# Two steps near the end of a fused attention and expert kernel change places, and the preparation of its leftover pair is reordered

## The chip, the cores and the metric

The kernel runs on one core of a Trainium2 chip. The metric is device time in microseconds (us), the median over runs. Engines are named as in the profile: PE (TensorE matmul, PEld its weight loads), DVE (VectorE), ACT (ScalarE), POOL (GpSimd), SP (SyncE, which here only issues transfers). A "q" behind an engine's name is its sequencer.

## What is computed

Eight batches of 384 tokens go through attention with 16 heads that share one set of keys and values. The result, as 3072 rows of 1024 numbers, goes through a two-stage gate: each row picks one of 4 groups, and in it one of 4 experts. Each row is then multiplied through its expert's two weight matrices.

```python
scores = scale * np.matmul(q, k.transpose(0, 1, 3, 2))      # q: 8 x 16 x 384 x 64, k: 8 x 1 x 384 x 64
attn = softmax(scores)
x = np.matmul(attn, v)                                       # reshaped to 3072 x 1024
g_idx = argmax(x @ w_group); e_idx = argmax(xg @ w_expert[g])
h = np.maximum(xg[mask_e] @ w1[g, e], 0.0)
out[tok_idx] = combined[:, None] * (h @ w2[g, e])            # combined: the product of both gate weights
```

With these inputs nearly all tokens of a batch choose the same expert. The kernel relies on that, and has a path for what is left over.

## The kernel before, in words

**Pairs.** The attention is cut into 24 steps that the code numbers `p`; p = 3b + st is third `st` (128 tokens) of batch `b`. Two consecutive steps are interleaved: the loop body of line 576 computes the scores of step p (`scores`, PE, then an exponential on ACT) while it multiplies the weights of the step before it with the values (`values`, PE). Scores and values alternate in six blocks j = 0 to 5. DVE adds up the exponentials (`pre_add`, five additions of 128x1024), inverts the sums (`invert`), and at the end of the body `weigh` scales the finished attention output of the step before: DVE writes it in fp32 to the tile `xT` (line 300), POOL casts it to bf16 in the tile `xbf` (line 301). After the last third of a batch, SP stores `xbf` to the DRAM buffer `x_bf`.

**Tiles that matter.** `xT` is one tile for all batches, overwritten third by third. `xbf` has two buffers, one per batch in turn. The PSUM tiles of scores, gates, counts and expert products all rotate through three buffers (`side`).

**Expert units.** For each batch the expert that the first 128 tokens choose most often is applied to all 384 tokens. That is 14 units of PE work (`moe_units`, line 398): 8 `h_unit`s (first matrix, 8 matmuls of 128x384 each, whose moving operand is the whole `xbf` of the batch) and 6 `y_unit`s (second matrix). `fill(n)` runs the next n units. They are run in phases behind every third step (`PHASES`, line 523): behind step 3b + 1 the 14 units of batch b - 1. Behind step 22, the last phase, only the 8 h units of batch 6 are run (line 525). Its 6 y units and all 14 units of batch 7 follow behind the loop, around the values of the last step and the leftover pair.

**Gate.** `gate_a(b, lo, hi)` is 64 small matmuls over thirds lo to hi of `xT`. `choose_a` and `counts(b, None)` find the expert of batch b from its first third (DVE, PE, ACT, DVE), and `choose_b` (line 349) has POOL read the index and issue the loads of both weight matrices (four pieces of `w1`, one `w2`). `gate_math` computes the gate of all three thirds and `gate_c`, called by `counts(None, b)`, what goes with the chosen expert. In a phase, one `gates(b)` serves both: `xT` then holds the first third of batch b and the other two of batch b - 1.

**Leftover pair.** `early_pair` (line 536) picks one pair of batch and expert that has tokens left over. Its weights are loaded by `leftover_w1` and `leftover_w2`. Behind the loop the tokens of that batch are read back from `x_bf` into the tile `xe` (line 656); the up to 32 tokens concerned are ranked (`pr`, `rk`, `pick`, `pg`), gathered (`pb` transposes, `px`), sent through both matrices (`ph`, `py`) and scattered to their rows. All this is written out by hand between `fill` calls, so that an engine's queue holds exactly the order of the code. Two computations that belong to a safety check, `bound_a` and `bound_b` (two transposes `pq` on PE), stand among it.

The program ends with three more units, an indirect store of the leftover rows (line 755), and a branch that is not taken here.

## Time and profile before

| | |
|---|---|
| median of 3 runs | 463.39 us (463.28 to 463.78) |
| span of the profiled execution | 462.4 us |
| PE busy | 449.4 us (97%) |
| DVE busy | 308.8 us (67%) |
| ACT busy | 241.6 us (52%) |
| POOL busy | 60.4 us (13%) |
| last matmul ends | 454.59 us |

The profile page gives busy times by engine and the costliest groups of instructions. In a timeline, each line has the start of a run of like instructions, its length, the engine, the line of the code, the tile written and those read, the count, and in brackets how long the engine stood idle before and for what. A line of the list of waits gives the total, the number and the longest. PE's busy time is modelled and pipelined matmuls overlap, so a group's cost is best read as the distance from its start to the start of the next group.

### The profile page before, as it was taken

The numbers are of one execution on the slowest core, as the hardware profiler recorded it, in microseconds if no ns is written. First come the engines' busy times: TensorE is split into PE (matmuls) and PEld (weight loads), VectorE is DVE, ScalarE is ACT, GpSimd is POOL, SyncE is SP. The second block draws the span as 40 slices with busy tenths as digits, with TensorE's granted clock in tenths as the row PEclk, the third lists the DMA queues.
The fourth block names the chain that finished last, engine by engine and source line by source line (L and its number), as shares of the span: only waits on it lengthen the run. The fifth ranks groups of instructions, "written<-read, shape, count | busy, mean of one in ns | idle before, by whom it ended". The sixth has DMA issues, their size and how long they took to land. (4 is left out here: it accounts for less than half of the span.)

```text
span 462.4 us, 10190 instructions
## 1 busy us (share of the span) xinstructions
PE 449.4 (97%) x4196; PEld 200.4 (43%) x4208; DVE 308.8 (67%) x489; ACT 241.6 (52%) x345; POOL 60.4 (13%) x83
## 2 busy tenths in 40 slices
PE   8999999999999999999999999999999999999893
PEld 6334445333643345433543336433453335434551
DVE  4899965499708985199834997089852999554511
ACT  2966643676347743566436763477435664532231
POOL 1004003000210103000030002101030001501000
PEclk9999999999999999999999999999999999999998
DMA  8688997997599296993979566992969910999952
GB/s 164 92 141 116 217 215 106 262 191 150 95 197 251 53 205 93 246 197 89 152 121 272 109 139 106 216 243 44 199 100 252 188 69 2 162 217 268 270 134 104
DMA packets 152454, 74.55 MB, mean 161 GB/s; under 512 B 120256, under 2 KB 138944, under 8 KB 152400
## 3 DMA queue, kind: packets, MB, share of 16 engines
q0 software_dynamic: 28416, 37.81, 48.0%
q1 hardware_dynamic: 122656, 35.68, 33.0%
q8 instruction: 35, 0.57, 0.5%
q10 hardware_dynamic: 1328, 0.33, 0.4%
q14 instruction: 19, 0.16, 0.1%
HBM read 92.62 MB, written 19.01 MB: 241 GB/s over the span
## 5 line engine op out<-in xcount | busy, mean ns | idle before, releaser
L253 ACT ACTIVATE pt<-s 128x1024 f32<-128x1024 f32 x144 | 142.1, 1026 | 71.9 <-PE s L251 71.2
L251 PE MATMUL s<-qT,kT 64*64 64x512 f32 x1152 | 142.4, 594 | 0.3 <-ACT qT L229 0.2
L290 PE MATMUL o<-pt,v 64*64 64x512 f32 x1152 | 141.1, 590 | 0.0
L261 DVE TENSOR_TENSOR presum<-presum,pt 128x1024 f32<-128x1024 f32 x96 | 116.6, 1215 | 15.2 <-ACT pt L253 9.8
L407 PE MATMUL hps<-xbf,w 128*128 128x384 bf16 x512 | 87.3, 326 | 0.4 <-ACT hT L408 0.4
L417 PE MATMUL yps<-w,hT 128*128 128x512 bf16 (+1 forms) x380 | 84.6, 375 | 0.6
L259 DVE TENSOR_TENSOR presum<-pt 128x1024 f32<-128x1024 f32 x24 | 29.4, 1223 | 76.8 <-ACT pt L253 75.4
L290 PEld LDWEIGHTS o<-pt,v 64*64 64x64 f32 x1152 | 43.4, 133 | 76.8 <-issue 73.0
L251 PEld LDWEIGHTS s<-qT,kT 64*64 64x64 f32 x1152 | 40.8, 133 | 66.8 <-issue 60.0
L407 PEld LDWEIGHTS <-w 128*128 128x128 bf16 x512 | 48.1, 98 | 38.1 <-issue 7.3
L301 POOL CAST xbf<-xT 128x1024 bf16<-128x1024 f32 x24 | 25.0, 1041 | 302.7 <-DVE xT L300 302.7
L419 ACT ACTIVATE y<-yps,gsel 128x512 f32<-128x512 f32 x46 | 31.6, 687 | 56.9 <-PE yps L417 55.3
L408 ACT ACTIVATE hT<-hps 128x384 bf16<-128x384 f32 x64 | 31.2, 488 | 55.6 <-PE hps L407 52.4
L417 PEld LDWEIGHTS <-hT 128*128 128x128 bf16 x392 | 37.7, 98 | 44.6 <-issue 2.4
L145 POOL DMA_DIRECT2D w<-in_moe_w_dram x36 | 24.8, 707 | 58.1 <-DVE gsel L395 37.7
L300 DVE TENSOR_TENSOR xT<-o,rinv 128x1024 f32<-128x1024 f32 x24 | 29.2, 1215 | 2.5 <-PE o L290 2.5
L280 DVE STREAM_TRANSPOSE rinv<-rc 128x1024 f32<-128x1024 f32 x24 | 29.9, 1245 | 0.8
L265 DVE TRANSPOSE_TENSOR_REDUCE fold<-presum 128x32 f32<-128x1024 f32 x24 | 29.6, 1232 | 0.0
L243 DVE STREAM_TRANSPOSE qT<-qraw 128x1024 f32<-128x1024 f32 x20 | 23.6, 1202 | 0.0
L209 ACT ACTIVATE qraw<-qraw 128x1024 f32<-128x1024 f32 x21 | 22.0, 1049 | 0.0
L273 PEld LDWEIGHTS sm<-fold,sel 64*64 64x64 f32 x192 | 7.3, 133 | 13.3 <-issue 13.3
L312 PE MATMUL gps<-xT,gw 128*32 128x96 f32 (+2 forms) x576 | 12.6, 239 | 0.0
(152 smaller groups left out, 152.9 us busy)
## 6 DMA issues: line engine op xcount, KB each, us to landing
w<-in_moe_w_dram POOLq DMA_DIRECT2D x36, 512.0 KB, 11.3
w<-in_moe_w_dram POOLq DMA_DIRECT2D x9, 2048.0 KB, 25.9
out_dram<-y SPq DMA_DIRECT2D x23, 512.0 KB, 6.9
qraw<-in_q_dram SPq DMA_DIRECT2D x56, 192.0 KB, 3.6
x_bf<-xbf SPq DMA_DIRECT2D x8, 768.0 KB, 4.0
v<-in_v_dram SPq DMA_DIRECT2D x16, 96.0 KB, 3.1
k<-in_k_dram SPq DMA_DIRECT2D x28, 48.0 KB, 2.7
qn<-in_q_dram SPq DMA_DIRECT2D x4, 256.0 KB, 5.2
```

Of the source, the lines that this page charges most:

```text
L251: nc.tensor.matmul(out=ps[64 * c:64 * c + 64, a, :], lhsT=kT[b][r, j * D:(j + 1) * D], rhs=qT[p][r, c * CW:(c + 1) * CW], start=True, stop ...
L253: nc.scalar.activation(out=t[:], in_=ps[:], func=ACTF.Exp, scale=scale)
L259: nc.vector.tensor_add(out=presum[p][:], in0=pt[p, 0][:], in1=pt[p, 1][:])
L261: nc.vector.tensor_add(out=presum[p][:], in0=presum[p][:], in1=pt[p, j][:])
L265: nc.vector.tensor_reduce(out=fold[p][:], in_=presum[p][:].rearrange("p a (n i) -> p (a n) i", i=32), axis=AX, op=OP.add, apply_transpose= ...
L280: nc.vector.transpose(out=t[:].rearrange("p (b i) -> p b i", i=32), in_=rc[:].rearrange("p c b -> p (c b)").unsqueeze(2).to_broadcast([P, ...
L290: nc.tensor.matmul(out=o_ps[p][64 * a:64 * a + 64, c, :], lhsT=v_sb[b][r, j, :], rhs=pt[p, j][r, a, :], start=(j == 0), stop=(j == KB - 1))
L300: nc.vector.tensor_mul(out=xT[b][:, :, ts], in0=o_ps[p][:].rearrange("p c (h n) -> p (c h) n", n=P), in1=rinv[p][:].rearrange("p (h n) -> ...
L407: nc.tensor.matmul(out=ps[:, 0:S], lhsT=w1[:, ko, fc * P:(fc + 1) * P], rhs=xb[:, ko, :], start=(ko == 0), stop=(ko == KO - 1))
L408: nc.scalar.activation(out=state["h"][:, fc, :], in_=ps[:, 0:S], func=ACTF.Relu)
L417: nc.tensor.matmul(out=ps[:], lhsT=state["h"][:, fo, st * P:(st + 1) * P], rhs=w2[:, fo, cs], start=(fo == 0), stop=(fo == FO - 1))
L419: nc.scalar.activation(out=y, in_=ps[:], func=ACTF.Copy, scale=gs_of()[:, st:st + 1])
```

## The change

Steps 20 and 21 change places: the first third of batch 7 now runs before the last third of batch 6. The choice of batch 7's expert moves from the last phase into the body of step 22, in the form that step 2 already has for batch 0. With this the loads of its weights can be issued earlier, and only the rest of batch 6's gate stays in the phase.

```diff
+    def rest_of_gates(b):
+        gate_logits(b, gate_a(b, 1, ST), 1, ST)
+        gate_math(b)
...
-    for p in range(NP):
+    order = list(range(NP - 4)) + [NP - 3, NP - 4, NP - 2, NP - 1]
+    for prev, p in zip([None] + order, order):
         b, st = divmod(p, ST)
-        jobs = [lambda: gates(0), lambda: None, lambda: counts(0, None)] if p == 2 else []
+        jobs = []
+        if p == 2 or p == NP - 2:
+            jobs = [lambda: choose_a(b, gate_a(b, 0, 1)), lambda: None, lambda: counts(b, None)]
...
             if b == B - 1:
-                steps = {1: lambda: gates(b), 2: lambda: counts(b, None), 3: lambda: (counts(None, b - 1), early_pair())}
+                steps = {2: lambda: rest_of_gates(b - 1), 4: lambda: (counts(None, b - 1), early_pair())}
```

Everywhere else in the loop `p - 1` becomes `prev`. Behind the loop the preparation of the leftover pair is put in another order, so that each step on PE has at least one unit of other work between it and the step that makes its input:

```diff
-    fill(3)
+    bound_a()
+    fill(2)
+    bound_b()
+    fill(1)
     for j in range(KB):
...
     weigh(NP - 1)
     last = B - 1
-    fill(2)
-    gate_logits(last, gate_a(last, 1, ST), 1, ST)
-    gate_math(last)
-    bound_a()
-    fill(2)
-    counts(None, last)
-    bound_b()
-
     xe = pool.tile([P, KO, S], BF16, tag="qraw", bufs=2, name="xe")
     nc.sync.dma_start(out=xe[:].rearrange("p k s -> p (k s)"), in_=xb_dram[bass.ds(leftover["b"], 1)].rearrange("a p k -> (a p) k"))
+    fill(2)
+    rest_of_gates(last)
...
-    nfl = pool.tile([P, 1], FP32, tag="nfl", bufs=1, name="nfl")
-    nc.vector.reduce_sum(out=nfl[:], in_=extra[:], axis=AX)
-    fill(1)
+    fill(2)
     pr = side([P, CW], FP32, "pr")
...
+    of_last = pool.tile([P, 2, P], FP32, tag="presum", bufs=1, name="of_last")
+    nc.vector.tensor_scalar(out=of_last[:, 0, :], in0=pick[:, ST - 1, :], scalar1=leftover["final"][:, 0:1], scalar2=None, op0=OP.mult)
     pick_bf = pool.tile([P, ST, CAP], BF16, tag="kT", name="pick_bf")
     nc.vector.tensor_copy(out=pick_bf[:], in_=pick[:, :, 0:CAP])
...
-    fill(2)
+    fill(1)
+    counts(None, last)
+    nfl = pool.tile([P, 1], FP32, tag="nfl", bufs=1, name="nfl")
+    nc.vector.reduce_sum(out=nfl[:], in_=extra[:], axis=AX)
+    fill(1)
     pg = side([P, CW], FP32, "pg")
     for st in range(ST):
         nc.tensor.matmul(out=pg[:, 0:2], lhsT=pick[:, st, :], rhs=gi[:, st, :], start=(st == 0), stop=(st == ST - 1))
+    nc.tensor.transpose(out=pg[:, P:2 * P], in_=of_last[:, 0, :], identity=ident[:])
...
-    nc.tensor.transpose(out=pg[:, P:2 * P], in_=of_last[:, 0, :], identity=ident[:])
...
-    fill(1)
     xtok = []
     for st in range(ST):
+        fill(1)
         pb = side([P, Dm], BF16, "pb")
...
-        fill(1)
-    assert len(units) == 2 * ST
+    fill(1)
     px = side([P, KO, CAP], FP32, "px")
...
     leftover["yc"] = yc
-    fill(1)
+    fill(2)
     spread()
```

## The prediction

> **What bounds the kernel now.** I read the page's busy times first, then PE's list of waits, then the timeline around the two places the diff touches.

> ```profile
> PE 449.4 (97%) x4196; PEld 200.4 (43%) x4208; DVE 308.8 (67%) x489; ACT 241.6 (52%) x345; POOL 60.4 (13%) x83
> ```
> ```profile
> PE pr L672 <- DVE mb L664: 1.2, 1, 1.2
> PE pb L717 <- DMA xe<-x_bf: 0.8, 1, 0.8
> PE hps L407 <- ACT hT L408: 0.4, 1, 0.4
> PE pg L698 <- DVE gc L694: 0.4, 1, 0.4
> ```

> PE is the bound: past the first 8 us it waits four times, 2.8 us in all, and all four lie in the leftover preparation. So time changes only by PE work added, by these waits closed, or by a new wait on PE. The tail behind the loop on PE:

> ```profile
> 421.12 1.10 PE L312 MATMUL gps<-xT,gw 128*32 128x64 f32 x64
> 422.15 1.90 PE L417 MATMUL yps<-w,hT 128*128 128x512 bf16 x7
> ...
> 425.21 0.38 PE L512 MATMUL pq<-ident,sq 128*1 128x128 f32 x2
> 425.99 1.46 PE L407 MATMUL hps<-xbf,w 128*128 128x384 bf16 x8 [0.39 <-ACT hT L408]
> 428.65 0.18 PE L672 MATMUL pr<-mb,prefix 128*128 128x4 bf16 x1 [1.20 <-DVE mb L664]
> ...
> 432.69 0.33 PE L698 MATMUL pg<-ident,of_last 128*128 128x128 f32 x1 [0.37 <-DVE gc L694]
> ...
> 435.15 0.62 PE L717 MATMUL pb<-ident_bf,xe 128*128 128x128 bf16 x8 [0.83 <-DMA xe<-x_bf]
> ```

> The body of step 22 and the phase behind it, where PE never stops:

> ```profile
> 373.62 2.75 PE L251 MATMUL s<-qT,kT 64*64 64x512 f32 x24
> ...
> 384.15 2.77 PE L407 MATMUL hps<-xbf,w 128*128 128x384 bf16 x16
> 386.85 1.53 PE L312 MATMUL gps<-xT,gw 128*32 128x96 f32 x64
> 388.31 1.47 PE L407 MATMUL hps<-xbf,w 128*128 128x384 bf16 x8
> ```

> The body takes 384.15 - 373.62 = 10.53 us. The first h unit of batch 6 starts at once, because that batch's last third was weighed a whole body earlier. At the end of this body DVE and POOL weigh step 21:

> ```profile
> 384.79 1.22 DVE L300 TENSOR_TENSOR xT<-o,rinv 128x1024 f32<-128x1024 f32 x1
> ```
> ```profile
> 386.07 1.04 POOL L301 CAST xbf<-xT 128x1024 bf16<-128x1024 f32 x1 [9.38 <-DVE xT L300]
> ```

> The cast ends at 387.11, 2.96 us after PE has left the body. Nobody needs it there now.

> [...] So a waiting first h unit holds everything behind it; the trace agrees, PE's groups follow the code's order. [...] Here the last matmul ends at 454.59 and the granted clock still is 1.00 up to 459, then 0.62 in the next microsecond, so it fell about 4.6 us later; a gap of 3 us should not trip it. [...] All 24 casts took 1.04 us[...].

> **Part 1, the swap: a new wait.** Now step 20 precedes step 22, so the body of step 22 ends with the weighing of step 20, the last third of batch 6. The h units of batch 6 follow directly and read all of `xbf`. PE must stand until values -> xT -> cast is done. Nothing else is queued ahead of that unit on PE; all 8 h units, the gate and the next step's scores stand behind it.

> **Part 2, the choice moved into step 22.** Step 2 has the same body with the same jobs, so I read its price there:

> ```profile
> 26.67 2.75 PE L251 MATMUL s<-qT,kT 64*64 64x512 f32 x24
> 29.36 0.76 PE L312 MATMUL gps<-xT,gw 128*32 128x32 f32 x64
> ...
> 33.65 0.18 PE L338 MATMUL cps<-ohe,ones_bf 128*128 128x16 bf16 x1
> ```
> ```profile
> 38.02 1.18 DVE L261 TENSOR_TENSOR presum<-presum,pt 128x1024 f32<-128x1024 f32 x1
> ```

> Step 2's body runs from 26.67 to 39.59, 12.92 us. From it I take the transposes `qps` that step 22 lacks (36.80 to 37.82, and 0.11 for the switch): 11.8 us. Against 10.53 that is +1.27: 0.69 for the gate's matmuls, 0.11 for the count, 0.17 where the last scores wait for a PSUM buffer, the rest in changes of shape.

> On DVE, step 2's last addition starts 11.35 us into the body and ends at 12.5. In step 22 the chain is the same (choice 0.75, index 0.46, five additions, inversion), so xT runs from 12.5 to 13.7 and the cast from 13.75 to 14.8. POOL must first issue batch 7's five loads: in step 2 the index was ready 8.75 into the body and POOL finished issuing at 13.96; in six of the other seven batches it finished 4.7 after the index, here 13.45. So POOL is free between 13.45 and 13.96, and the cast ends between 14.8 and 15.05. I take 14.8, and 0.1 for the hand-over: the first h unit starts 14.9 into the body instead of 10.53, **+4.35 us**, of which 1.27 is Part 2 and 3.1 idle PE (bounds 2.7, if DVE gains 0.4 on step 2, and 3.4).

> **Part 3, the phase.** The gate of 96 columns (386.85 to 388.31, 1.46) becomes one of 64 (421.12 to 422.15, 1.03): **-0.43**. Its input, xT of step 20, is there three h units earlier. `early_pair` moves back one unit; its DVE work ends about where the phase ends, and step 23's first addition comes 3 us later, so nothing waits.

> **Part 4, the earlier loads.** Today batch 7's loads are issued from 392.78 and the leftover weights queue behind them. No weight tile is in PE's list of waits, so arriving 9 us sooner is worth nothing by itself. It empties the DMA engines before the tail, which is where `x_bf` (7.8 us to land there, 3.4 at best) and `xe` (7.0) were slow.

> **Part 5, the tail.** Start to start: `pq` 425.21 to 425.99 is 0.78, alone some 0.35, so -0.4. h at 425.99 plus 1.30 is 427.29, `pr` at 428.65: -1.35. `pg` to its transpose 431.59 to 432.69 is 1.10, in one go some 0.65: -0.45. h at 432.85 plus 1.30, `pb` at 435.15: -1.0. Sum 3.2. Does each close? `pr` now comes one y and one h unit (1.74 + 1.30) behind the gate. DVE's chain from gate to `mb` is 2.2 us (422.28 to 424.51) and another 0.65 (428.01 to 428.59, with the hand-over), 2.9 after 422.28, so `mb` is there at the moment PE arrives: closed, with 0.1 to spare at most. `xe` is issued when `x_bf` has landed: 3.5 + 4 us behind the store, about 428 in the old tail's time against a `pb` at 430.5: closed if the transfers run as on an empty bus. I take **-3.1**, with bounds -2.3 (xe late by 0.8) and -3.4. What follows `y` unit 3 (spread, two units, the indirect store) keeps its order and its 12 us.

> **Sum:** +4.35 - 0.43 - 3.1 = +0.82, so 463.39 + 0.8 = **464.2 us**, 0.17% more.

> **Rivals.** *Slower:* the cast has to wait for POOL's loads (+0.25), and the tail closes only 2.3, for `xe` or `mb` (+0.8): +1.9, 465.3 us. For it: step 2's slow issue, and `mb` without slack. Against it: six of the eight issues are quicker and the DMA engines are less loaded. *Faster:* PE does not wait for the cast, because something I overlook fills the gap, and only +1.27 - 0.43 - 3.1 = -2.3 remains, 461.1 us. For it: PE has not one such idle stretch now. Against it: the h unit's operand is the whole `xbf`, and no unit of batch 5 is left at that point (its 14 are used up behind step 19). *Loads decide:* if batch 7's weights had been the limit, the swap would pay; the list of waits has no such line, so I give it nothing apart from `xe`.

> **How the numbers follow.** The balanced case has 70% and spreads over 463.5 to 464.9 with the bounds of Parts 2 and 5. The bound of 0.2% is 0.93 us, that is 464.32, just above its middle: 0.46 of it count as no change and 0.24 as slower. The slower rival has 20%, the faster one 8%, and 2% are left for what I don't see (no change). Chances: faster 0.08, no change 0.48, slower 0.44. The range goes from 463.0 to 465.4; the faster rival and half of the outer slower cases lie outside.

> **What would show it.** Right: PE's list of waits has a new line of about 3 us, h unit on POOL's cast, right behind step 22; the phase behind is 0.4 shorter; the four waits of the tail are gone, or under 0.3 in sum; the loads start near 383.5. Wrong: no such wait, or a wait over 3.6 with a fallen clock; `pb` still on `xe`; a new wait of `py` on the second leftover weights, which are now needed some 5 us sooner after their issue.

## The result, and the profile after

The changed kernel takes 466.26 us (median of 6 runs, 465.43 to 466.8) against 463.58 us before (463.08 to 463.78): ratio 1.0058, 95% interval 1.0046 to 1.0071. It is slower by 2.7 us, outside the range of 463.0 to 465.4 that was forecast. The profiled execution is the quickest of the six, with a span of 463.9 us (465.43 us of device time) against 462.4 (463.94) before.

First the busy times of the profile after, then PE's list of waits behind the first 8 us (total, times, longest):

```profile
PE 450.4 (97%) x4272; PEld 200.4 (43%) x4272; DVE 308.3 (66%) x489; ACT 241.9 (52%) x345; POOL 60.5 (13%) x83
```
```profile
PE hps L407 <- POOL xbf L301: 2.9, 1, 2.9
PE py L749 <- DMA w<-in_moe_w_dram: 1.5, 1, 1.5
```

The four waits of the tail are gone. Two others stand in their place: the first h unit of batch 6 on POOL's cast, and `py`, the leftover pair's second product, on its weights.

PE's timeline in the body of step 22 and the phase behind it:

```profile
373.69 2.75 PE L251 MATMUL s<-qT,kT 64*64 64x512 f32 x24
376.38 0.76 PE L312 MATMUL gps<-xT,gw 128*32 128x32 f32 x64
...
380.67 0.18 PE L338 MATMUL cps<-ohe,ones_bf 128*128 128x16 bf16 x1
...
388.51 4.06 PE L407 MATMUL hps<-xbf,w 128*128 128x384 bf16 x24 [2.91 <-POOL xbf L301]
392.50 1.10 PE L312 MATMUL gps<-xT,gw 128*32 128x64 f32 x64
...
400.16 2.81 PE L251 MATMUL s<-qT,kT 64*64 64x512 f32 x24
```

What it waits for, in DVE's and then in POOL's timeline:

```profile
386.14 1.21 DVE L300 TENSOR_TENSOR xT<-o,rinv 128x1024 f32<-128x1024 f32 x1
```
```profile
383.49 2.73 POOL L145 DMA_DIRECT2D w<-in_moe_w_dram  x4 [6.72 <-issue]
386.18 0.93 POOL L357 DMA_DIRECT2D w<-in_moe_w_dram  x1
387.41 1.04 POOL L301 CAST xbf<-xT 128x1024 bf16<-128x1024 f32 x1 [0.31 <-DVE xT L300]
```

The first h unit starts 388.51 - 373.69 = 14.82 us into the body; before it was 10.53. The next step's scores begin at 400.16, which is 3.90 us later than in the kernel before:

```profile
396.26 2.81 PE L251 MATMUL s<-qT,kT 64*64 64x512 f32 x24
```

POOL was done with its five loads at 387.11, and xT was ready at 387.35, so the loads did not hold the cast.

The tail on PE's timeline:

```profile
425.23 1.10 PE L312 MATMUL gps<-xT,gw 128*32 128x64 f32 x64
...
429.31 0.18 PE L671 MATMUL pr<-mb,prefix 128*128 128x4 bf16 x1
...
434.30 0.61 PE L718 MATMUL pb<-ident_bf,xe 128*128 128x128 bf16 x8
...
444.38 1.89 PE L417 MATMUL yps<-w,hT 128*128 128x512 bf16 x8
447.79 1.06 PE L749 MATMUL py<-w,hc 128*32 128x256 bf16 x32 [1.53 <-DMA w<-in_moe_w_dram]
...
452.99 3.65 PE L417 MATMUL yps<-w,hT 128*128 128x512 bf16 x24
```

The load that `py` waits for, on POOL's timeline, and the time from its issue to its landing, after and before:

```profile
428.99 0.89 POOL L575 DMA_DIRECT2D w<-in_moe_w_dram  x1 [4.79 <-PE yps L417]
```
```profile
DMA to landing us min/median/max: 18.7/18.7/18.7
```
```profile
DMA to landing us min/median/max: 20.8/20.8/20.8
```

`pr` and `pb` no longer wait. A y unit takes 1.74 us, so PE was ready for `py` at 446.12 and lost 1.67. From the scores of step 23 to the end of the last matmul it is 400.16 to 456.64, 56.48 us; before it was 396.26 to 454.59, 58.33. The tail thus gained 1.85: 3.5 from the closed waits, less 1.67. With the loop's 3.90 the last matmul comes 2.05 later. What follows it took 7.3 us instead of 7.8, which leaves the span's +1.5.

That is not the 2.7 us of the medians. Of the 1.2 us between them, 0.4 is that the profiled execution of the kernel before was itself slower than its median (463.94 against 463.58). The other 0.8 is in the list of the six executions. Each has a mean granted clock, the share of TensorE's full speed that the profile records, averaged over the execution. The profiled one, at 465.43, has 0.998; the others take 465.91 to 466.80 at 0.991 to 0.994. The experiments had to say what costs that clock.

### The profile page after: what moved, and what is told of

Read it like the earlier page. It is cut to its first block, busy times and chain, and to the rows that moved or that the text cites. A ratio compares the mean times of both kernels' runs of the same rounds, so it can differ in the third digit from the quotient of the medians.

```text
span 463.9 us, 10326 instructions
## 1 busy us (share of the span) xinstructions
PE 450.4 (97%) x4272; PEld 200.4 (43%) x4272; DVE 308.3 (66%) x489; ACT 241.9 (52%) x345; POOL 60.5 (13%) x83
## 5 line engine op out<-in xcount | busy, mean ns | idle before, releaser
L251 PE MATMUL s<-qT,kT 64*64 64x512 f32 x1152 | 142.7, 594 | 0.0
L261 DVE TENSOR_TENSOR presum<-presum,pt 128x1024 f32<-128x1024 f32 x96 | 116.6, 1215 | 14.9 <-ACT pt L253 9.5
L407 PE MATMUL hps<-xbf,w 128*128 128x384 bf16 x512 | 87.2, 326 | 2.9 <-POOL xbf L301 2.9
L417 PE MATMUL yps<-w,hT 128*128 128x512 bf16 (+1 forms) x392 | 85.2, 375 | 0.0
L251 PEld LDWEIGHTS s<-qT,kT 64*64 64x64 f32 x1152 | 40.8, 133 | 66.9 <-issue 60.2
L407 PEld LDWEIGHTS <-w 128*128 128x128 bf16 x512 | 48.1, 98 | 40.3 <-issue 9.6
L301 POOL CAST xbf<-xT 128x1024 bf16<-128x1024 f32 x24 | 25.0, 1043 | 293.7 <-DVE xT L300 293.7
L408 ACT ACTIVATE hT<-hps 128x384 bf16<-128x384 f32 x64 | 31.3, 489 | 56.1 <-PE hps L407 51.4
L417 PEld LDWEIGHTS <-hT 128*128 128x128 bf16 x392 | 37.8, 98 | 44.6 <-issue 2.4
L300 DVE TENSOR_TENSOR xT<-o,rinv 128x1024 f32<-128x1024 f32 x24 | 29.2, 1215 | 2.5 <-PE o L290 2.5
L318 DVE STREAM_TRANSPOSE L<-gps 128x32 f32<-128x32 f32 (+1 forms) x16 | 3.7, 228 | 16.5 <-PE gps L312 16.5
```

Source lines behind the costliest of these rows:

```text
L251: nc.tensor.matmul(out=ps[64 * c:64 * c + 64, a, :], lhsT=kT[b][r, j * D:(j + 1) * D], rhs=qT[p][r, c * CW:(c + 1) * CW], start=True, stop ...
L261: nc.vector.tensor_add(out=presum[p][:], in0=presum[p][:], in1=pt[p, j][:])
L300: nc.vector.tensor_mul(out=xT[b][:, :, ts], in0=o_ps[p][:].rearrange("p c (h n) -> p (c h) n", n=P), in1=rinv[p][:].rearrange("p (h n) -> ...
L407: nc.tensor.matmul(out=ps[:, 0:S], lhsT=w1[:, ko, fc * P:(fc + 1) * P], rhs=xb[:, ko, :], start=(ko == 0), stop=(ko == KO - 1))
L408: nc.scalar.activation(out=state["h"][:, fc, :], in_=ps[:, 0:S], func=ACTF.Relu)
L417: nc.tensor.matmul(out=ps[:], lhsT=state["h"][:, fo, st * P:(st + 1) * P], rhs=w2[:, fo, cs], start=(fo == 0), stop=(fo == FO - 1))
```

## The experiments

The theory after the result: PE's pieces are +3.90 in the loop, -3.5 in the tail and +1.7 for the new wait of `py`; on top of it, the idle stretch of 2.9 us at the cast makes the granted clock fall in many executions, against what the prediction had said. The rival: the additional time and the lower clock come from elsewhere. "Before" is each time the kernel before, run beside the experiments on the same chip.

**The changed kernel once more,** without an edit.

> The changed kernel once more, unaltered. In its first trace PE's pieces sum to +2.05 us at the last matmul (loop and phase +3.90, new wait of py on the second leftover weights +1.6, tail gaps -3.45) and the span grows by 1.5 us, but the median over six runs grew by 2.7 us, and the runs with more time show a lower mean clock (0.991 to 0.994 against 0.998). Theory: PE's new idle stretches let the granted clock fall for a few us in most executions; then the median is again 466 to 466.6, and a run with a clock near 0.992 shows matmuls at half speed right behind one of the two waits. Rival: the extra 0.8 us has nothing to do with these waits (the end of the program, other work on the chip); then the clock falls elsewhere or not at all while the time stays near 466.3.

Measured: 466.39 us (463.65 to 467.81, 8 runs) against 463.79, ratio 1.0048 (1.0027 to 1.0069). This time the profiled execution is one with a low clock, 0.991. PE's timeline and wait, and busy times by stretches of 2 us (PE, PEld, DVE, ACT, POOL, granted clock, DMA share, GB/s):

```profile
388.87 5.47 PE L407 MATMUL hps<-xbf,w 128*128 128x384 bf16 x24 [2.90 <-POOL xbf L301]
394.27 1.10 PE L312 MATMUL gps<-xT,gw 128*32 128x64 f32 x64
```
```profile
388.00:390.00 2.00, 1.13 (x4) 0.55 (x4) 1.99 (x2) 0.00 (x0) 0.82 (x1) 0.59 1.14 179
390.00:392.00 2.00, 2.00 (x8) 0.96 (x7) 0.00 (x0) 0.38 (x1) 0.00 (x0) 0.56 1.10 158
```
```profile
PE py L749 <- DMA w<-in_moe_w_dram: 0.2, 1, 0.2
```

The three h units behind the wait take 394.27 - 388.87 = 5.40 us instead of 3.99: the clock is at about half between 388 and 392, and nowhere else before the end of the program. That is the theory's picture. Not all eight executions fit it: the slowest, 467.81 us, has a clock of 0.995, and its excess is not explained. Two with a clock of 0.996 take 463.65 and 464.18, about as long as the kernel before.

The `py` wait is 0.2 here instead of 1.5. `pr` comes 1.76 us later than in the first trace (431.07 against 429.31), `py` only 0.48 (448.27 against 447.79). If the issue of its weights moved with `pr`, they landed some 17.4 us behind it instead of 18.7, an estimate from these starts (18.7 - 1.76 + 0.48); why is not shown.

**Only the loop's part.** The tail is that of the kernel before; the edit is shown against that kernel.

```diff
-    for p in range(NP):
+    order = list(range(NP - 4)) + [NP - 3, NP - 4, NP - 2, NP - 1]
+    for prev, p in zip([None] + order, order):
...
-                steps = {1: lambda: gates(b), 2: lambda: counts(b, None), 3: lambda: (counts(None, b - 1), early_pair())}
+                steps = {2: lambda: rest_of_gates(b - 1), 4: lambda: (counts(None, b - 1), early_pair())}
```

> Only the loop's part of the change: steps 20 and 21 swapped, the choice moved into step 22, the tail as before. Theory: loop and phase +3.9 us, of it 2.9 idle on the cast; the earlier loads free the DMA engines, so the wait of pb on xe (1.0 with its start) goes, and py has its old 22 us behind the issue of its weights, so it does not wait: 463.6 + 2.9 = 466.5 us by the pieces, and 467.3 if the idle stretch at the cast is what costs clock. Rival (the clock is lost at the py wait): 466.5 with a clock as in the kernel before.

Measured: 467.22 us (465.78 to 470.15, 6 runs), ratio 1.0087 (1.0065 to 1.0109). Three executions have a clock of 0.997 or more and take 465.8 to 466.7, three have 0.992 or 0.993 and take 467.7 to 470.2. From the profiled execution (clock 0.998), PE's timeline:

```profile
388.58 4.06 PE L407 MATMUL hps<-xbf,w 128*128 128x384 bf16 x24 [2.91 <-POOL xbf L301]
...
438.12 0.61 PE L721 MATMUL pb<-ident_bf,xe 128*128 128x128 bf16 x8
...
450.44 1.06 PE L753 MATMUL py<-w,hc 128*32 128x256 bf16 x32
```

`pb` and `py` do not wait, and still the clock falls in half of the executions. So the wait of `py` is not needed for the fall. By itself the loop's part loses 3.4 us, as the theory had it with the clock.

**Only the tail's part.** The loop is that of the kernel before; the edit is shown against the changed kernel.

```diff
-    order = list(range(NP - 4)) + [NP - 3, NP - 4, NP - 2, NP - 1]
-    for prev, p in zip([None] + order, order):
+    for p in range(NP):
...
```

> Only the tail's reordering, the loop as before, so no swap, no early choice. Theory: the tail's waits on hT, mb and gc close (-2.4 us), pb on xe perhaps not, as the leftover weights still queue behind batch 7's, and py arrives some 3 us before its weights, which landed at 445.7 before: net between -0.3 and +0.7, 463.3 to 464.3 us, with a wait of py of 2 to 3 us. Rival (the earlier loads buy nothing in the tail): all four waits close and py does not wait, 460.2 us.

Measured: 466.98 us (466.39 to 468.2, 6 runs), ratio 1.0075 (1.0061 to 1.0089). The theory missed by about 3 us and the rival by almost 7. PE's timeline, SP's timeline, and the stretches of 2 us:

```profile
435.95 0.62 PE L718 MATMUL pb<-ident_bf,xe 128*128 128x128 bf16 x8 [4.79 <-DMA xe<-x_bf]
436.40 2.66 PE L407 MATMUL hps<-xbf,w 128*128 128x384 bf16 x8
438.86 1.06 PE L718 MATMUL pb<-ident_bf,xe 128*128 128x128 bf16 x8
```
```profile
420.92 0.33 SPq L303 DMA_DIRECT2D x_bf<-xbf  x1
428.59 0.36 SPq L655 DMA_DIRECT2D xe<-x_bf  x1
```
```profile
436.00:438.00 2.00, 2.00 (x14) 1.19 (x15) 0.69 (x1) 0.00 (x0) 0.00 (x0) 0.63 1.07 305
```

`x_bf` lands 7.5 us behind its issue and `xe` 7.3 behind its own, much as before (7.8 and 7.0): the DMA share is 1.06 to 1.25 in every stretch of 2 us from 410 to 436, where in the changed kernel it is 0.00 to 0.52 from 422 to 428. In the trace before, the last piece of the leftover `w1`, issued at 398.97, took 36.7 us to land. But the new order asks for `xe` at 431.0. So PE waits 4.8 us where it waited 0.8, and behind that the clock is at half again: an h unit takes 2.46 instead of 1.30. I had taken the old wait of 0.8 as what was at stake; the tail's other gains only bring PE to the same transfer earlier. The two halves of the change need each other: in the changed kernel `x_bf` lands in 3.4 us, `xe` in 5.2, and `pb` finds it.

**One y unit ahead of `py`.** The changed kernel, with the unit that it had moved behind `py` put back in front.

```diff
     nc.vector.tensor_copy(out=hc[:], in_=phT[:])
-    fill(1)
+    fill(2)
...
     leftover["yc"] = yc
-    fill(2)
+    fill(1)
```

> The changed kernel with one y unit (1.74 us) moved from behind py to ahead of it, where it stood before. Theory: py comes 1.74 us later than today and its weights have landed, so the wait of 1.5 is gone and nothing is added: 466.3 - 1.6 = 464.7 us. If the py wait is also what costs clock, 463.9. Rival (the weights are later when other work precedes them, or the store of the middle third, now issued at the same place, sets the end): no more than 0.5 us gained, 465.8.

Measured: 465.83 us (463.68 to 466.43, 6 runs), ratio 1.0047 (1.0034 to 1.0060). The profiled execution has a clock of 0.997 and is the one at 463.68; the five others have 0.991 to 0.993. On PE's timeline the wait is gone:

```profile
444.38 3.62 PE L417 MATMUL yps<-w,hT 128*128 128x512 bf16 x16
447.93 1.06 PE L749 MATMUL py<-w,hc 128*32 128x256 bf16 x32
```

The median is that of the rival (465.8), though not for its reason: the wait did go, but the clock still falls. The edit is worth hardly 0.6 us on the median, measured beside the changed kernel's 466.39. In the three traces with both halves of the change and no y unit put back (the changed kernel's two, and the one below with PE kept busy) the wait of `py` is 1.5, 0.2 and 0.3 us; the 1.5 of the first trace, which the theory counted on, is the upper end. To see executions with and without a fallen clock side by side the kernel was run again.

> The kernel with the y unit ahead of py once more, for a trace of an execution in which the clock fell: five of its six executions took 465.6 to 466.4 us at a clock of 0.991 to 0.993, the sixth 463.7 at 0.997. Theory: all of the 2.2 us between them is h units at half clock behind the wait for the cast; three h units then take some 6 us instead of 4.0 and nothing later differs. Rival: the half clock costs only the 1.4 us seen in the changed kernel's second trace, and the other 0.8 lies elsewhere, in a second fall or in transfers that land later.

Measured: 464.67 us (463.36 to 466.62, 20 runs), ratio 1.0024 (1.0009 to 1.0038). Ten executions have a clock of 0.996 or more and take 463.36 to 464.38, ten have 0.990 to 0.994 and take 464.95 to 466.62. Their medians are 463.57 and 466.07: executions with a fallen clock take 2.5 us longer here. The profiled one had a full clock, so the question of this run, where the part beyond the 1.4 us seen in the h units lies, stays open.

**PE kept busy in the wait.** The changed kernel with matmuls that nobody reads, placed into PE's wait for the cast.

```diff
             if b == B - 1:
+                busy = side([P, CW], FP32, "busy")
+                for _ in range(44):
+                    nc.tensor.matmul(out=busy[:, 0:P], lhsT=ones_bf[:], rhs=ones_bf[:], start=True, stop=True)
                 steps = {2: lambda: rest_of_gates(b - 1), 4: lambda: (counts(None, b - 1), early_pair())}
```

> The changed kernel with 44 extra matmuls of 128x128 ones into a PSUM tile that nobody reads, ahead of the first h unit of batch 6, some 2.5 us that fit into PE's 2.9 us of waiting for the cast. No useful work is moved. Theory (the idle PE lets the granted clock fall to half, for some 3.4 us, in most executions): the clock is 0.997 or more in all executions and the time that of the changed kernel's best traces, 465.0 to 465.6 us. Rival (the clock falls for another reason, or the spread comes from elsewhere): clocks of 0.991 to 0.994 and a median of 466.4 as before.

Measured: 464.97 us (463.45 to 466.3, 12 runs) against 463.40, ratio 1.0030 (1.0018 to 1.0042). Clocks are 0.994 to 0.997 in all twelve: eight of them below the 0.997 of the theory, but none at 0.993 or lower, where 8 of the 14 executions of the changed kernel lie.

```profile
386.20 2.63 PE L638 MATMUL busy<-ones_bf 128*128 128x128 bf16 x44
389.18 4.06 PE L407 MATMUL hps<-xbf,w 128*128 128x384 bf16 x24 [0.35 <-POOL xbf L301]
```

The cast ends no sooner and no useful work is moved, yet the loss shrinks from 2.6 or 2.7 us to 1.6. The idle PE was what lowered the clock. That the clock was some 1.1 us of the changed kernel's median is less firm: the interval of the loss here overlaps that of the second series (1.0027 to 1.0069). The `py` wait is 0.3 in this trace, as in the trace with the fallen clock. The twelve executions still spread over 2.9 us, so the clock is not the only thing that varies.

**The gate into the wait,** on top of the kernel with the y unit ahead of `py`.

```diff
-                steps = {2: lambda: rest_of_gates(b - 1), 4: lambda: (counts(None, b - 1), early_pair())}
+                rest_of_gates(b - 1)
+                steps = {4: lambda: (counts(None, b - 1), early_pair())}
```

> On top of the kernel with the y unit ahead of py (462.2 us span without a fallen clock, 465.8 us median): the rest of batch 6's gate moves ahead of the first h unit. It needs xT but not the cast, so its 1.03 us fall into the wait. Theory: PE's idle stretch shrinks from 2.9 to about 1.8 us, which is 1.0 us less by the pieces, 462.7 us where the clock holds; if a stretch of 1.8 us is too short to lower the clock, that is the median, otherwise 464.5. Rival (the wait ends later because DVE's gate work now precedes nothing useful): no gain, 465.8.

Measured: 462.93 us (462.12 to 464.87, 14 runs), ratio 0.9994 (0.9982 to 1.0006). The lowest clock is 0.994.

```profile
388.01 1.10 PE L312 MATMUL gps<-xT,gw 128*32 128x64 f32 x64 [1.89 <-DVE xT L300]
389.05 6.67 PE L407 MATMUL hps<-xbf,w 128*128 128x384 bf16 x40
```

The gate needs only xT, so it runs while POOL casts, and the h units follow it without a gap. The time is near the 462.7 us that the theory gave for a clock that holds. An idle stretch of 1.9 us did not bring the clock down to 0.993 in any of the 14 executions; two of them, at 0.994, took 464.8 and 464.87 us, which is not explained.

**Two y units of batch 5 into the wait,** on top of the same kernel. The load of batch 7's second weights, which takes the buffer that these units read, is issued behind them.

```diff
-    PHASES[NP - 2] = FO
+    PHASES[NP - 5] -= 2
+    PHASES[NP - 2] = FO + 2
...
+        def rest():
+            w2 = wpool.tile([P, FO, Dm], BF16, tag="w2", name="w2")
+            nc.gpsimd.dma_start(out=w2[:], in_=w2f[bass.ds(reg, 1)].rearrange("a p k f -> (a p) k f"))
+            wts[b][1] = w2
...
-                steps = {2: lambda: rest_of_gates(b - 1), 4: lambda: (counts(None, b - 1), early_pair())}
+                steps = {1: lambda: late.pop()(), 4: lambda: rest_of_gates(b - 1), 6: lambda: (counts(None, b - 1), early_pair())}
```

> On top of the kernel with the y unit ahead of py: two y units of batch 5 are held back from the phase behind step 19 to the start of the phase behind step 22, 3.5 us of useful PE work for the 2.9 us of waiting; the load of batch 7's second weights, which needs the buffer these units read, is issued behind them. Theory: the wait on the cast is gone, -2.9 us by the pieces, and the clock holds: 463.7 - 2.9 = 460.8 us, better than the kernel before by 2.9. Rival (holding back the load of the second weights pushes the leftover weights back and xe or py waits again): 462 to 463.7.

Measured: 460.60 us (460.15 to 461.51, 5 runs) against 463.40, ratio 0.9942 (0.9929 to 0.9955). PE's and POOL's timelines:

```profile
382.71 3.63 PE L426 MATMUL yps<-w,hT 128*128 128x512 bf16 x15
386.17 4.06 PE L416 MATMUL hps<-xbf,w 128*128 128x384 bf16 x24
```
```profile
384.59 1.04 POOL L301 CAST xbf<-xT 128x1024 bf16<-128x1024 f32 x1 [1.19 <-DVE xT L300]
386.64 0.89 POOL L363 DMA_DIRECT2D w<-in_moe_w_dram  x1 [1.00 <-PE yps L426]
```

The cast ends at 385.63, while the held-back units still run, and the h units start without a wait. In the tail nothing waits either. This version is 2.8 us faster than the kernel before, where the change as it was made is 2.7 slower, and within 0.2 of what was expected.

## Why the prediction was wrong

*Part 1 and Part 2, right.* The new wait was on POOL's cast, at the place named and of the size worked out from step 2: first h unit 14.82 us into the body against 14.9 forecast, +4.29 against +4.35, 2.9 us idle against 3.1. POOL issued its loads in 3.62 us (383.49 to 387.11), as in six of the eight batches before (3.61 or 3.62), against 3.85 in step 2. The waiting unit did hold what stands behind it: the gate, whose xT was there at 387.35, ran at 392.50.

*Part 3, right.* Loop and phase together +3.90 against +3.92.

*Part 5, right in its gaps.* All four waits closed, for 3.5 us against 3.1; `mb` and `xe` were there in time, `mb` without slack as worked out (DVE's copy of what `pr` reads first ends at 429.25, `pr` starts at 429.31), `xe` at 432.9 for a `pb` at 434.30.

*The sum lacked a term.* The prediction saw that `py` now comes some 5 us sooner behind the issue of its weights, and named it only among the things that would prove it wrong, at no cost. PE reached `py` 17.1 us behind the issue (446.12 - 428.99); the weights landed 18.7 us behind it in the first trace (20.8 before) and, by the estimate from the starts, some 17.4 in two others: a wait of 1.5 us in the first, 0.2 to 0.3 in the others. The 20.8 of the trace before against the 17 us left was reason enough to give it a price. Putting one y unit back removed the wait, but took hardly 0.6 us off the median: this is the smaller of the two terms.

*The clock, wrong.* The step "a gap of 3 us should not trip it" failed. It took the 4.6 us after which the clock fell at the program's end for a safe length. It is not: in 25 of the 46 executions with 2.9 us of idle PE at this place the mean clock was 0.993 or less, and in the trace of such an execution the clock fell 2.4 us into the wait and stayed at half for 3.4 us. Keeping PE busy in that very gap kept the clock up (0.994 to 0.997 in all twelve executions), and the loss was some 1.1 us smaller. The 4.6 us was one draw: in the ten traces the clock falls between 2.0 and 5.2 us behind the last matmul. Whether a gap of this length lowers the clock differs between executions of one kernel; an estimate of why stands in the last section.

*Part 4, half right.* That the earlier loads are worth something only through `xe` held. Their worth was too small: with the new tail and the old loop `pb` waits 4.8 us, not 0.8, and the clock behind it is at half for 3.4 us.

The working gives +0.8, less the 0.4 that the tail gained beyond its forecast. With 0.2 to 1.5 for `py` and 1.1 for the clock that is +1.7 to +3.0, against 2.7 measured; how the 2.7 of the median divide between the two terms is not shown more closely.

## What to carry to other kernels

With PE busy 97% of the span, an idle stretch of 2.9 us had two prices here: its length, and, in 25 of 46 executions, a mean clock of 0.993 or less. One trace with a full clock (the first, at 0.998) did not show that the gap was harmless. Fill a gap of 3 us with work that is there anyway, taken from an earlier phase; here two units held back, together with the y unit ahead of `py`, turned a loss of 2.7 us into a gain of 2.8. When a wait is closed by reordering, set each transfer's issue against its new time of use, not against the old wait: the waits that were closed here led straight to the next transfer (`py` 1.5 us on its weights, `pb` 4.8 on `xe` with the tail alone).

## What the runs showed that I had not expected

The granted clock at an idle PE. Of 52 executions of kernels with an idle stretch of 2.9 us or more in the middle, 29 had a mean clock of 0.993 or less; of 92 without one (the kernel before among them, and the one with 1.9 us), none had. In the kernel that was run 20 times it was ten low (one of them at 0.994) and ten high, 2.5 us apart.

Why it falls in some executions only is my estimate from these times and PE's timelines. As changes 20, 133 and 134 steps apart still lie on whole steps, it counts steps of 3.413 us from a change that is seen through the rest of the trace. Cut so, a trace falls into stretches, and how long PE was busy in one goes with the clock of the next. These are the cases nearest to the limit:

| trace | stretch (us) | PE busy in it (us) | clock in the next |
|---|---|---|---|
| changed kernel once more | 384.94 to 388.35 | 1.03 | half |
| only the tail's part, behind the last matmul | 456.98 to 460.40 | 1.37 | half |
| only the tail's part | 429.68 to 433.09 | 1.48 | full |
| gate into the wait | 385.50 to 388.91 | 1.52 | full |
| one y unit ahead of `py` | 384.04 to 387.45 | 1.58 | full |
| changed kernel, first trace, behind the last matmul | 455.02 to 458.44 | 1.61 | full |
| changed kernel, first trace | 386.76 to 390.17 | 1.66 | full |

From 384 us on, no stretch of the ten traces breaks the order: up to 1.37 us of busy PE the next one is at half clock, from 1.48 on at full. By this estimate the clock falls when some 2 us of idle PE lie in one stretch (2.04 in the second row, 1.93 in the third). Of the 2.90 us of waiting in the changed kernel's second trace 2.38 lie in one, of the 2.91 in its first at most 1.75; the 1.89 us with the gate in the wait are shorter than 2. The limit rests on these few traces, and PE's busy time in them is modelled.

Of the 2.5 us between low and high executions, the two traces of the changed kernel account for 1.4 in the three h units behind the wait. Another 0.36 had been lost before 383 us already, where the last values ahead of the wait begin at 383.21 instead of 382.85; where the rest goes is not shown.
